# Another order of all engine queues in the expert steps of a fused attention, mixture-of-experts and FFN kernel

## The chip, the cores and the metric
The kernel runs on one core of a Trainium2 chip. The metric is the device time of one execution in microseconds. An engine takes its instructions in the order in which the program lists them: TensorE (PE, with weight loads as PEld), VectorE (DVE), ScalarE (ACT), GpSimd (POOL) and SyncE (SP), which here issues most DMA transfers. The engines meet at semaphores.

## The reference: what is computed
Three parts, all in fp32, on 4608 tokens of 512 features.

```
attn[b,h] = softmax_d(q) @ (softmax_s(k)^T @ v)            # 8 x 8 heads, 576 x 64
x = attn as 4608 x 512
e = argmax(x @ w_gate);  g = softmax(x @ w_gate)[e] * sigmoid(x @ w_output_gate)[e]
y[t] = g[t] * relu(x[t] @ w1[e[t]]) @ w2[e[t]]             # 8 experts, 512 -> 1024 -> 512
h = y @ w_in;  out = (h * cos(h)) @ w_out                  # 512 -> 2048 -> 512
```

## The kernel before, in words
Every fp32 product is made of three matmuls on a high and a low part of each operand (high x high, low x high, high x low); the low part of the hidden activations stands beside the high one. So before a weight or a token block can be used, ACT rounds it to its high part and DVE (or POOL) subtracts that to get the low one.

The kernel has three stages: attention with the router, the expert stage, and the FFN. The change is in the expert stage. After the router, the tokens are sorted by expert: DVE works out each token's position ("pos", L942 to L955), makes one-hot matrices from its low and high digits ("low", "hot", "ri": L186, L966 to L974), PE multiplies these in three groups of 12 (L978) to the list of token numbers in sorted order, and two DVE instructions ("inv", L981 and L982) make the integer list by which POOL gathers. "far" (L960 to L962) checks with one tiny matmul whether a position lies beyond a bound.

The expert stage then runs 22 steps, numbered 0 to 21, after the string "DDDHDHFDHDHDHFF". Each F is a step of 256 tokens (two blocks of 128), each D a pair of them that share one expert's weights, each H a half step of 128 tokens. That makes 17 full steps and 5 half steps: 6, 9, 13, 16 and 19 are the half ones. A step takes this way through the engines, with the lines by which the profile names it:

- weights: "ld" loads a quarter of an expert's two matrices (SP, L256), "wh" makes the high part (ACT, L264), "wl" the low one (DVE, L268; the fourth quarter for the first step, raw tile 3, on POOL);
- tokens: "gat" gathers a block of 128 (POOL, L277, two buffers), "norm" scales it (POOL, L282), "tr" transposes it (PE, L287), "xh" and "xl" make the two parts (ACT L294, DVE L299);
- first product: "mm0" and "mm1" (PE, L1141 to L1144) for each of four groups of hidden columns, "hh" the relu and high part (ACT, L1162), "hl" the low part (DVE, L1166), "hs" a sum for half steps;
- second product: "mm2" (PE, L1177 to L1179), "y" copies and stores it (ACT, L1183 and L1185).

Steps 0 and 1 gather tokens before the sort is finished, by a list known earlier; from step 2 on the gather needs "inv".

Beside this, the stage prepares the FFN's weights, which arrive as double floats and are taken apart with integer instructions: "cld" (SP load), "csq" and "clf" (ACT, L1063, L1066), "ca", "ch", "cp" (DVE, L1071 to L1079), "cm", "cs" (POOL, L1082, L1086), "cw" (DVE, L1099). From the result "wsum" (POOL, L1114) adds combinations, "whi" and "wlo" split them (ACT L1122, DVE L1126), "wst" stores them (a DMA issued by ACT, L1129).

All of this is written as a table of operations: a name, a key (a planned time in us), the function that emits the instructions, and the names of operations that have to be emitted earlier. One routine emits them: of all operations whose listed ones are out, it takes the one with the smallest key. This fixes the order of every engine's queue. Two examples of entries, "hh" and "hl" of step j and group n, and the sort's "far":

```
("far", ST["far"], s_far, "pos"),
...
op(T0 + (bt["dmm1"] * n + 0.3 if j else 0.3) if soon else t1 + bt["hh"], ("hh", j, n), ..., ("mm1", j, n), ...)
```

## Time and profile before

| | us |
|---|---|
| median of 3 runs (lowest, highest) | 1468.21 (1467.05, 1470.45) |
| the profiled execution | 1465.47 |
| its span | 1463.7 |
| attention and router, 0 to 185.06 | 185.06 |
| expert stage, 185.06 to 684.11 | 499.05 |
| FFN, 684.11 to 1463.70 | 779.59 |

The span is the time from the first to the last instruction that the profiler saw; the rest of the profiled execution's time lies around it. The expert stage is counted from the first matmul of step 0's first product to the first one of the FFN, and a step from its first such matmul to that of the next.

### The profile page before, as it was taken

Reading aid. Unit: us, or ns where it says so; the run is one execution under the profiler, and the core shown is the slowest. Engines: PE = TensorE matmul, PEld = TensorE weight load, DVE = VectorE, ACT = ScalarE, POOL = GpSimd, SP = SyncE. Lnnn points to the kernel's source line nnn. Section 1 sums busy time; section 2 is a strip of 40 time slices with the busy share of each in tenths; the row PEclk is TensorE's granted clock in tenths of the full one; section 3 lists DMA queues with packets and bytes.
Section 4 is the critical chain, followed back from the end, with each engine's and each line's share of the span. In section 5 each row is a group of like instructions: output and inputs, shape, how many; then the busy total and the mean of one; then the engine's idle time right before and its main releaser. Section 6 shows DMA issues by size and latency. Waiting matters only on the chain.

```text
span 1463.7 us, 25384 instructions
## 1 busy us (share of the span) xinstructions
PE 1396.7 (95%) x9530; PEld 1241.4 (85%) x9530; DVE 983.2 (67%) x1465; ACT 872.8 (60%) x1613; POOL 545.2 (37%) x391
## 2 busy tenths in 40 slices
PE   6898869999899999899999999999999999999998
PEld 5777759899799889799898898988889899898887
DVE  7999985777787888786655655546565554655544
ACT  3776515456464655566766666666666666666654
POOL 5555314564644463624252423406032240603000
PEclk9999889999999999999999999999999999999999
DMA  9985424767886967897667575666657566665662
GB/s 314 278 263 168 157 96 143 275 249 246 295 289 244 315 228 249 309 300 253 226 184 220 173 230 169 210 193 197 204 172 231 170 200 200 202 202 171 192 192 82
DMA packets 189731, 317.99 MB, mean 217 GB/s; under 512 B 27744, under 2 KB 60000, under 8 KB 189600
## 3 DMA queue, kind: packets, MB, share of 16 engines
q1 hardware_dynamic: 153760, 253.54, 54.9%
q10 hardware_dynamic: 29840, 42.92, 8.0%
q0 software_dynamic: 6000, 19.83, 4.2%
q8 instruction: 78, 1.28, 0.4%
q14 instruction: 53, 0.43, 0.1%
HBM read 264.17 MB, written 52.05 MB: 216 GB/s over the span
## 4 chain that ended last, share of the span: by engine, by line
PE 52%; ACT 2%; DVE 2%; issue 1%; POOL 0%; DMA 0%; ACTq 0%
PE acc L1574 8%; PE acc L1572 8%; PE acc L1573 8%; PE bank L1508 7%; PE bank L1510 7%; PE bank L1509 7%; DVE n L1542 1%; PE p L1473 1%; PE yps L1177 1%; PE yps L1178 1%; PE yps L1179 1%; DVE n L1551 1%; PE hp L1144 1%; PE hp L1141 1%; ACT n L1545 1%
## 5 line engine op out<-in xcount | busy, mean ns | idle before, releaser
L1508 PE MATMUL bank<-xo,wp 128*128 128x256 f32 x994 | 281.6, 283 | 1.5 <-ACT part L1522 0.6
L1510 PE MATMUL bank<-xo,wp 128*128 128x256 f32 x994 | 277.6, 279 | 0.0
L1509 PE MATMUL bank<-xo,wp 128*128 128x256 f32 x994 | 277.2, 279 | 0.0
L1551 DVE SCALAR_TENSOR_TENSOR n<-n,h 128x512 f32<-128x512 f32 x144 | 126.0, 875 | 171.1 <-ACT n L1548 171.1
L1572 PE MATMUL acc<-wh,ht 128*128 128x512 f32 x576 | 227.6, 395 | 0.2 <-ACT ht L1557 0.2
L1573 PE MATMUL acc<-wl,ht 128*128 128x512 f32 x576 | 227.4, 395 | 0.0
L1574 PE MATMUL acc<-wh,ht 128*128 128x512 f32 x576 | 226.8, 394 | 0.5 <-DVE ht L1561 0.5
L1508 PEld LDWEIGHTS bank<-xo,wp 128*128 128x128 f32 x994 | 186.8, 188 | 22.8 <-ACT part L1522 4.2
L1509 PEld LDWEIGHTS bank<-xo,wp 128*128 128x128 f32 x994 | 186.7, 188 | 16.2
L1141 PE MATMUL hp<-xTh,wh 128*128 128x256 f32 x704 | 187.8, 278 | 2.9 <-DVE ht L1166 2.9
L1144 PE MATMUL hp<-xTh,wl 128*128 128x256 f32 x704 | 187.4, 277 | 0.0
L1510 PEld LDWEIGHTS bank<-xo,wp 128*128 128x128 f32 x994 | 187.4, 189 | 0.0
L268 DVE TENSOR_TENSOR wl<-raw,wh 128x1024 fp32r<-128x1024 f32 x121 | 168.8, 1419 | 26.4 <-ACT wh L264 26.4
L857 POOL TENSOR_TENSOR xo<-x,xo 128x512 fp32r<-128x512 f32 x24 | 31.1, 1298 | 373.3 <-ACT xo L852 373.3
L1530 DVE TENSOR_TENSOR h<-bank,part 128x256 f32<-128x256 f32 x213 | 89.3, 421 | 111.4 <-PE bank L1510 110.4
L264 ACT CAST wh<-raw 128x1024 fp32r<-128x1024 f32 x126 | 127.5, 1053 | 42.5 <-PE yps L1179 25.8
L1537 ACT ACTIVATE n<-h 128x512 int32<-128x512 f32 x144 | 91.1, 632 | 101.4 <-DVE h L1530 97.8
L1143 PE MATMUL hp<-xTl,wh 128*128 128x256 f32 x544 | 150.8, 277 | 0.0
L1545 ACT ACTIVATE n<-n 128x512 f32<-128x512 f32 x144 | 91.2, 633 | 77.9 <-DVE n L1542 77.9
L1141 PEld LDWEIGHTS hp<-xTh,wh 128*128 128x128 f32 x704 | 132.2, 188 | 4.5 <-DVE ht L1166 3.5
L1144 PEld LDWEIGHTS hp<-xTh,wl 128*128 128x128 f32 x704 | 132.2, 188 | 0.2
L1574 PEld LDWEIGHTS acc<-wh,ht 128*128 128x128 f32 x576 | 108.3, 188 | 26.7 <-DVE ht L1561 1.4
(310 smaller groups left out, 3093.8 us busy)
## 6 DMA issues: line engine op xcount, KB each, us to landing
wp<-ws SPq DMA_DIRECT2D x504, 256.0 KB, 2.8
raw<-in_moe_w_dram SPq DMA_DIRECT2D x60, 1024.0 KB, 7.2
ws<-wst ACTq DMA_DIRECT2D x28, 512.0 KB, 6.1
...
```

The source lines that it names most:

```text
L264: sc.copy(out=wh[j, c][:, s], in_=rawt[c][:, s])
L268: eng.tensor_tensor(out=wl[j, c][:, s], in0=rawt[c][:, s], in1=wh[j, c][:, s], op=ALU.subtract)
L1141: pe.matmul(hp[:, f2, :], w_h, xTh[j][:, d, :], start=(d == 0), stop=False)
L1143: pe.matmul(hp[:, f2, :], w_h, xTl[j][:, d, :], start=False, stop=False)
L1144: pe.matmul(hp[:, f2, :], w_l, xTh[j][:, d, :], start=False, stop=(d == KD - 1))
L1508: pe.matmul(h, w[:, 0, k], x[:, i, 0, k], start=(first and k == 0), stop=False, skip_group_check=True)
L1509: pe.matmul(h, w[:, 0, k], x[:, i, 1, k], start=False, stop=False, skip_group_check=True)
L1510: pe.matmul(h, w[:, 1, k], x[:, i, 0, k], start=False, stop=(k == 1), skip_group_check=True)
L1551: ve.scalar_tensor_tensor(out=rs[j, s], in0=rs[j, s], scalar=-0.5, in1=hs[j, s], op0=ALU.add, op1=ALU.mult)
L1572: pe.matmul(acc[t, a], gh[f][:, ts], w_h, start=(c == 0), stop=False)
L1573: pe.matmul(acc[t, a], gh[f][:, ts], w_l, start=False, stop=False)
L1574: pe.matmul(acc[t, a], gl[f][:, ts], w_h, start=False, stop=(c == KF - 1))
```

## The change
A table SHIFT gives an offset to the keys, by the operation's name and its place: the kind of step (the first of a pair is "D", the second or a single one "F", a half step "H"; for token blocks and weights that of the step before; steps 0 to 2 by number) and the block, group or quarter. The offsets are added just before the operations are emitted. Since dependences that the old keys implied no longer hold by themselves, they are now listed. No instruction is added, removed or changed; the last offsets also swap the order of a few parts of the FFN's first token tile.

```
-            op(c3 + n, ("wh", 3, n), lambda n=n: whigh(0, 3, n))
+            op(c3 + n, ("wh", 3, n), lambda n=n: whigh(0, 3, n), ("wh", 3, n - 1))
...
-                   ("xl",) + (pv2 or (-1, 0)))
+                   ("xl",) + (pv2 or (-1, 0)), ("tr",) + (tiles[-2] if len(tiles) > 1 else (-1, 0)))
...
-                       ("hl", j, 2 * c + 1), ("wl", 4 * g + 2 + c, 1),
+                       ("hl", j, 2 * c), ("hl", j, 2 * c + 1), ("wl", 4 * g + 2 + c, 0), ("wl", 4 * g + 2 + c, 1),
...
-        issue(ops)
+        SHIFT = dict(
...
+            cld={('i',): -3.65, ('o',): -18.9},
...
+            hh={('0', 2): 7.8, ('1', 2): -3, ('1', 3): -36.3, ('D', 0): 0.4, ('D', 1): 4.2, ('F', 2): -72.8, ('F', 3): -45.95,
+                ('H', 3): -1.05},
...
+            norm={('1', 0): -18.3, ('1', 1): 16.25, ('D', 0): -3.75, ('F', 0): -3.2, ('H', 0): 7.1},
...
+            s={('exp',): 14.15, ('gate',): 11.85, ('hot',): 15.45, ('mm_0',): 11.05, ('more',): 13.55, ('pos',): 16.35,
+                ('px',): 2},
+            tr={('D', 0): -68.85, ('F', 0): -1.55, ('H', 0): -100.5, ('H', 1): -76.35, ('Z', 2): 0.55},
...
+        def place(n):
...
+            if t in ("gat", "norm", "tr", "xh", "xl"):
+                return ("Z" if j == NSLOT else kinds[j - 1] if j > 2 else str(j), n[2])
+            if t in ("hh", "hl", "hs", "y"):
+                return (kinds[j] if j > 1 else str(j), n[2])
+            return (j,) if t in ("oh", "ol", "xs") else ()
+
+        issue({n: (key + SHIFT.get(n[0], {}).get(place(n), 0.0), fn, deps) for n, (key, fn, deps) in ops.items()})
```

What this does to the queues is shown at three places.

First, step 0 on DVE, after the position chain: one piece of the difference. L186 are the twelve compares of "low", L960 and L961 are "far", L299 a low part of step 1's tokens, L966 to L974 the one-hots, L1166 low parts of step 0's hidden groups 2 and 3.

```order
 L186 TENSOR_SCALAR ht<-iota_b,lo_f 128x128 x12
+L960 TENSOR_SCALAR fl<-posf 128x4
+L961 TENSOR_SCALAR posN<-posf 128x4
+L299 TENSOR_TENSOR xTl<-t,xTh 128x4x128
 L966 TENSOR_TENSOR ohh<-ht,hi_b 128x36x27 x2
 L968 TENSOR_SCALAR rpi<-ohh,pcol 128x36x54
 L974 TENSOR_TENSOR rpi<-ohh,iota_b 128x36x54
-L1166 SCALAR_TENSOR_TENSOR hx<-hp,hx 128x512 x2
-L299 TENSOR_TENSOR xTl<-t,xTh 128x4x128
-L960 TENSOR_SCALAR fl<-posf 128x4
-L961 TENSOR_SCALAR posN<-posf 128x4
```

"far" now stands behind the compares and ahead of the one-hots; the low parts of groups 2 and 3 are done ahead of the position chain.

On PE in the same step, the rows around "far" (L962). Before, it stands between the first and the second of four groups of twelve second products (yps is the block's accumulator):

```order
L1178 MATMUL yps_2521<-wl_2092,hx_2413 128x512
L1179 MATMUL yps_2521<-wh_2091,hx_2413 128x512
L962 LDWEIGHTS ones_c_81
L962 MATMUL sp_2277<-fl_2538,ones_c_81 1x4
L1177 MATMUL yps_2573<-wh_2091,hx_2385 128x512
L1178 MATMUL yps_2573<-wl_2092,hx_2385 128x512
```

Now it stands behind the last of them, and the first product of step 1 follows; the sort's matmuls, which stood between the other groups, are in step 1.

```order
L1178 MATMUL yps_2499<-wl_2307,hx_2478 128x512
L1179 MATMUL yps_2499<-wh_2306,hx_2478 128x512
L962 LDWEIGHTS ones_c_81
L962 MATMUL sp_2277<-fl_2583,ones_c_81 1x4
L1141 MATMUL hp_2595<-xTh_2481,wh_1936 128x256
L1143 MATMUL hp_2595<-xTl_2482,wh_1936 128x256
```

Second, step 7 on ACT: the relus of its hidden groups 1, 2 and 3 (L1162), two high parts of the prepared FFN weights (L1122), their stores (L1129), and one conversion (L1063, L1066). Before:

```order
L1162 ACTIVATE ht_4194<-hp_4167 128x512
L1122 CAST wst_4198<-wf_3632 128x2x2x128
L1122 CAST wst_4203<-wf_3632 128x2x2x128
L1129 DMA ws_133<-wst_4198 128x2x512
L1129 DMA ws_133<-wst_4203 128x2x512
L1063 ACTIVATE sq_4239<-rw_4152 128x512
L1066 ACTIVATE rw_4152<-rw_4152 128x512
L1162 ACTIVATE ht_4270<-hp_4206 128x512
```

Now the relu of group 2 follows that of group 1 directly, and the stores come behind that of group 3:

```order
L1162 ACTIVATE ht_4215<-hp_4160 128x512
L1162 ACTIVATE ht_4244<-hp_4190 128x512
L1063 ACTIVATE sq_4247<-rw_3937 128x512
L1066 ACTIVATE rw_3937<-rw_3937 128x512
L1122 CAST wst_4258<-wf_3681 128x2x2x128
L1122 CAST wst_4263<-wf_3681 128x2x2x128
L1162 ACTIVATE ht_4266<-hp_4219 128x512
L1129 DMA ws_133<-wst_4263 128x2x512
```

Third, step 8 on POOL: a gather for the half step 9 (L277), its scaling (L282), and conversions (L1082, L1086) and a sum (L1114) of the FFN's weights. Before:

```order
L277 DMA xg_4350<-xs_64,invI_2261 128x520
L1086 TENSOR_TENSOR rw_4235<-rw_4235 128x512
L1114 TENSOR_TENSOR wsum_4378<-wf_3632 128x512
L1082 TENSOR_TENSOR rw_4321<-rw_4321,a_4384 128x512
L1086 TENSOR_TENSOR rw_4321<-rw_4321 128x512
L1114 TENSOR_TENSOR wsum_4444<-wf_3632,wsum_4318 128x512
L282 TENSOR_TENSOR xg_4350<-xg_4350 128x4x128
```

Now one conversion less and one sum less stand between gather and scaling:

```order
L277 DMA xg_4326<-xs_64,invI_2261 128x520
L1114 TENSOR_TENSOR wsum_4352<-wf_3681 128x512
L1082 TENSOR_TENSOR rw_3937<-rw_3937,a_4316 128x512
L1086 TENSOR_TENSOR rw_3937<-rw_3937 128x512
L282 TENSOR_TENSOR xg_4326<-xg_4326 128x4x128
```

The scaling moved ahead of the last conversion and of a sum, which follow behind it.

And on PE ahead of step 7: behind the last second products of the half step 6 now come the transposes of step 8's first block (L287), which stood in the middle of step 7.

```order
L1178 MATMUL yps_4073<-wl_3963,ht_4066 128x512
L1179 MATMUL yps_4073<-wh_3962,ht_4067 128x512
L287 MATMUL t_4114<-ident_68,xg_4014 128x128 x4
L1141 MATMUL hp_4124<-xTh_4056,wh_3994 128x256
L1143 MATMUL hp_4124<-xTl_4057,wh_3994 128x256
```

The same move is made for the second step of five other pairs (steps 3, 5, 12, 15 and 18), and the transposes of the step behind a half step (7, 10, 14, 17, 20) moved from its second products into the middle of its first ones.

## Rows read from the trace of the kernel before

**Rows 1.** Windows: the expert stage; columns: start:end, us, busy us (count) by engine, clock, DMA share, GB/s.
```profile
185.06:684.11 499.05, 471.47 (x3093) 421.63 (x3093) 386.48 (x510) 264.93 (x408) 231.79 (x164) 0.98 0.72 249
```

**Rows 2.** The same view by step: steps 0, 2, 7, 8, 9 and 14.
```profile
185.06:224.75 39.69, 27.25 (x192) 23.93 (x191) 31.22 (x95) 7.42 (x13) 5.90 (x4) 0.83 0.27 94
...
247.51:270.50 22.99, 22.99 (x154) 20.82 (x153) 17.64 (x24) 11.03 (x19) 13.80 (x10) 1.00 0.47 159
...
355.16:383.11 27.95, 25.03 (x154) 21.78 (x152) 26.95 (x30) 15.17 (x24) 17.77 (x10) 0.94 0.63 223
383.11:407.91 24.80, 23.04 (x150) 20.42 (x148) 17.59 (x20) 12.48 (x18) 15.49 (x12) 1.00 0.93 327
407.91:421.66 13.75, 13.75 (x98) 12.61 (x97) 10.11 (x17) 9.80 (x18) 1.94 (x2) 1.00 0.97 337
...
507.32:534.23 26.91, 23.91 (x154) 20.47 (x152) 26.02 (x29) 15.83 (x25) 18.17 (x10) 1.00 0.64 221
```

**Rows 3.** Waits of PE in the expert stage: total us, times, longest.
```profile
PE yps L1177 <- ACT ht L1162: 7.1, 3, 2.9
PE t L287 <- POOL xg L282: 3.1, 5, 0.8
```

**Rows 4.** Timeline of PE in step 0: start, us, operation, [idle before, releaser].
```profile
212.30 0.16 PE L962 MATMUL sp<-fl,ones_c 128*1 128x4 bf16 x1 [12.44 <-DVE fl L960]
...
217.32 1.34 PE L978 MATMUL sp<-rpi,ht 128*128 128x108 bf16 x24
...
221.32 0.75 PE L978 MATMUL sp<-rpi,ht 128*128 128x108 bf16 x12
```

**Rows 5.** Windows: the stretch after PE's longest idle time in step 0.
```profile
212.39:216.84 4.45, 4.45 (x12) 3.48 (x12) 3.19 (x21) 0.47 (x2) 0.00 (x0) 0.50 0.77 251
```

**Rows 6.** Timeline of DVE in step 0.
```profile
193.37 0.43 DVE L942 TENSOR_TENSOR pa<-sp,lim 128x288 f32<-128x288 f32 x1
...
197.97 2.37 DVE L953 TENSOR_SCALAR lo_i<-posI 128x12 int32<-128x12 int32 x1
...
200.37 2.28 DVE L955 CAST lo_f<-lo_i 128x12 f32<-128x12 int32 x1
...
203.34 2.02 DVE L186 TENSOR_SCALAR ht<-iota_b,lo_f 128x128 bf16<-128x128 bf16 x12
205.29 2.23 DVE L966 TENSOR_TENSOR ohh<-ht,hi_b 128x972 bf16<-128x972 bf16 x2
...
208.20 2.18 DVE L974 TENSOR_TENSOR rpi<-ohh,iota_b 128x1944 bf16<-128x1944 bf16 x1
...
212.09 0.16 DVE L960 TENSOR_SCALAR fl<-posf 128x4 bf16<-128x4 f32 x1
```

**Rows 7.** Timeline of POOL before and in step 0, and in step 1.
```profile
197.87 4.76 POOL L268 TENSOR_TENSOR wl<-raw,wh 128x1024 fp32r<-128x1024 f32 x2 [10.95 <-ACT wh L264]
...
227.22 0.98 POOL L277 DMA_INDIRECT xg<-xs,invI  x1
...
230.66 1.04 POOL L282 TENSOR_TENSOR xg<-xg 128x512 f32<-128x512 f32 x1 [1.20 <-DMA xg<-xs,invI]
```

**Rows 8.** Timelines of ACT: a relu of step 0, then step 7 (q: DMA issue).
```profile
196.25 0.60 ACT L1162 ACTIVATE hx<-hp 128x512 fp32r<-128x512 f32 x1 [2.12 <-PE hp L1144]
...
371.72 2.07 ACTq L1129 DMA_DIRECT2D ws<-wst  x2
373.83 0.68 ACT L1063 ACTIVATE sq<-rw 128x512 f32<-128x512 f32 x1 [7.93 <-DVE wst L1126]
...
374.98 0.57 ACT L1162 ACTIVATE ht<-hp 128x512 fp32r<-128x512 f32 x1
```

**Rows 9.** Timeline of DVE in step 7.
```profile
370.16 3.22 DVE L1126 TENSOR_TENSOR wst<-wf,wst 128x512 fp32r<-128x512 f32 x2
...
376.52 0.69 DVE L1126 TENSOR_TENSOR wst<-wf,wst 128x512 fp32r<-128x512 f32 x1
```

**Rows 10.** Timeline of POOL in step 8.
```profile
394.67 1.49 POOL L282 TENSOR_TENSOR xg<-xg 128x512 f32<-128x512 f32 x1
```

More of the change, by code (lines that the diff above doesn't have):

```diff
@@ L1314 @@
                      ("a", c_a, [("cm", m - 1)]), ("h", c_h, [("csq", m)]), ("p", c_p, []), ("m", c_m, [("clf", m)]),
-                     ("s", c_s, []), ("w", c_w, [("csq", m), ("wlo", f - 2, 6)]), ("hi", c_hi, [])]
+                     ("s", c_s, []), ("w", c_w, [("csq", m), *[("wlo", f - 2, i) for i in range(7)]]), ("hi", c_hi, [])]
             last = None
             for n, fn, deps in chain if kind == "o" else chain[:-1]:
-                op(t1 + CT[n], ("c" + n, m), lambda fn=fn, m=m: fn(m), *deps, *([last] if last else []))
+                op(t1 + CT[n], ("c" + n, m), lambda fn=fn, m=m: fn(m), *deps, ("c" + n, m - 1), *([last] if last else []))
                 last = ("c" + n, m)
@@ L1326 @@
                 for i, n, late in WP["part"]:
-                    op(tj[n] + WP["hi"] + late, ("whi", f, i), lambda f=f, i=i: w_high(f, i), *full,
+                    op(tj[n] + WP["hi"] + late, ("whi", f, i), lambda f=f, i=i: w_high(f, i), *full, ("wlo", f - 1, i),
                        *[("wsum", f, k) for k in range(4)][:{1: 1, 3: 2, 5: 3, 4: 4}.get(i, 0)], ("wst", f - 1, i))
@@ L1344 @@
                 if g and lead[j] == j and (slot or c < 3):
-                    free = ("wl", L - 3, 1)
+                    free = [("wl", i, n) for i in (L - 3, L - 4) for n in range(2)]
                     store = [("chi", 2 * KD * c + KD + n) for n in range(KD)] if slot is None else []
-                    op(t0 + pt[f"w{c}"] - 12.0, ("ld", L), lambda slot=slot, c=c: wload(slot, c), free, ("ld", L - 1), ("s", "eI"), *store)
+                    op(t0 + pt[f"w{c}"] - 12.0, ("ld", L), lambda slot=slot, c=c: wload(slot, c), *free, ("ld", L - 1), ("s", "eI"), *store)
                     use = ("mm1", j - 1, 2 * c + 1) if c < 2 else ("mm2", j - 1, c - 2, pa_)
                     for n in range(2):
-                        op(t0 + pt[f"w{c}"] + n * pt["dn"], ("wh", L, n), lambda j=j, c=c, n=n: whigh(j, c, n), ("ld", L), use)
+                        op(t0 + pt[f"w{c}"] + n * pt["dn"], ("wh", L, n), lambda j=j, c=c, n=n: whigh(j, c, n), ("ld", L), use,
+                           ("wh", L, n - 1))
                         op(t0 + pt[f"w{c}"] + n * pt["dn"] + pt["dl"], ("wl", L, n), lambda j=j, c=c, n=n: wlow(j, c, n, ve),
@@ L1375 @@
                 op(t1 + bt["mm1"] - (0.0 if j else 0.01), ("mm0", j, n), lambda j=j, n=n, slot=slot: mm1(j, n, slot, (0,)),
-                   ("xl", j, na - 1), ("wl", 4 * g + c, 1), ("hl",) + pm, ("mm1", j, n - 1))
+                   *[("xl", j, a) for a in range(na)], ("wl", 4 * g + c, 0), ("wl", 4 * g + c, 1), ("hl",) + pm, ("mm1", j, n - 1))
                 op(t1 + bt["mm1"] + (0.0 if j else bt["dmm1"] / 2), ("mm1", j, n),
@@ L1392 @@
             for a in range(na):
-                op(T0 + bt["y"] + bt["dmm2"] * a, ("y", j, a), lambda j=j, a=a, slot=slot: yout(j, a, slot), ("mm2", j, 1, a), ("s", "done"))
+                op(T0 + bt["y"] + bt["dmm2"] * a, ("y", j, a), lambda j=j, a=a, slot=slot: yout(j, a, slot), ("mm2", j, 1, a), ("s", "done"),
+                   ("y", j, a - 1) if a else ("y", j - 1, len(blocks(slots[j - 1])) - 1))
             T0 += LEN[kind] if j else P0["len"]
@@ L1415 @@
             op(t0 + at + 0.7, ("ol", i), lambda i=i, e2=e2: x_low(0, i, e2), ("oh", i))
-        issue(ops)
+        SHIFT = dict(
+            chi={('o',): 12.7},
+            cld={('i',): -3.65, ('o',): -18.9},
+            cm={('i',): 11.5, ('o',): 10.7},
+            cp={('o',): 3.4},
+            csq={('i',): 1.55, ('o',): 1.9},
+            cw={('i',): 3.15, ('o',): 7.6},
+            gat={('2', 1): 10.85, ('D', 0): -15.4, ('H', 1): 9.1},
+            hh={('0', 2): 7.8, ('1', 2): -3, ('1', 3): -36.3, ('D', 0): 0.4, ('D', 1): 4.2, ('F', 2): -72.8, ('F', 3): -45.95,
+                ('H', 3): -1.05},
+            hl={('1', 1): 3.05, ('1', 3): -14.1, ('D', 2): 6.4, ('F', 2): -33.3, ('F', 3): -88.65, ('H', 3): -72.1},
+            hs={('H', 0): -80.25, ('H', 1): -138.15, ('H', 2): -3.05, ('H', 3): -91.25},
+            ld={('F', 2): -13.65},
+            norm={('1', 0): -18.3, ('1', 1): 16.25, ('D', 0): -3.75, ('F', 0): -3.2, ('H', 0): 7.1},
+            oh={(3,): 3.6, (4,): 25.85, (5,): 18.6},
+            s={('exp',): 14.15, ('gate',): 11.85, ('hot',): 15.45, ('mm_0',): 11.05, ('more',): 13.55, ('pos',): 16.35,
+                ('px',): 2},
+            tr={('D', 0): -68.85, ('F', 0): -1.55, ('H', 0): -100.5, ('H', 1): -76.35, ('Z', 2): 0.55},
+            wh={('1', 0, 0): -1.8, ('1', 2, 1): 5.25, ('F', 2, 0): -20.4, ('F', 2, 1): -0.95, ('F', 3, 0): 1.1, ('F', 3, 1):
+                0.85, ('H', 0, 0): -111.6, ('H', 0, 1): -36.8, ('H', 2, 0): -0.15, ('H', 2, 1): -3.4, ('w3', 0): -45.2, ('w3',
+                1): -18.25},
+            whi={(1,): 18.9, (2,): 17.9, (5,): 17.65},
+            wl={('1', 0, 0): 4.65, ('1', 1, 0): 4.25, ('1', 2, 0): 3.35, ('F', 2, 1): 2.45, ('H', 0, 0): -164.95, ('H', 1, 0):
+                -18, ('H', 1, 1): -7.45, ('H', 2, 0): -0.25, ('H', 3, 0): -1.25, ('w3', 0): -58.35},
+            wlo={(0,): 13.55, (3,): 16.2},
+            wst={(0,): 33.95, (1,): 29.4, (2,): 22.8, (3,): 31.35, (5,): 29.6},
+            wsum={(3,): 32},
+            xh={('1', 1): 8.75, ('D', 1): 5.6, ('F', 1): 5.65, ('H', 0): -32.35},
+            xl={('2', 0): -5.75, ('F', 0): 6, ('H', 0): -44.6},
+            xs={(0,): 4.7, (3,): 3.85},
+            y={('0', 0): 7.35, ('1', 0): 10.15, ('D', 1): 12.45, ('F', 0): 1.5, ('F', 1): -47.1, ('H', 0): 11.6},
+            zero={(): 9.55},
+        )
@@ new lines, in place @@
+        def place(n):
+            t, j = n[0], n[1]
+            if t == "s":
+                return (j.rstrip("0123456789") if j.startswith("low") else j,)
+            if t in ("wh", "wl", "ld"):
+                if j == 3:
+                    return ("w3", n[2])
+                b = next(b for b in group if group[b] == j // 4)
+                return ("1" if b == 2 else kinds[b - 1], j % 4, *n[2:])
+            if t in ("cld", "csq", "clf", "ca", "ch", "cp", "cm", "cs", "cw", "chi"):
+                return (cjobs[j][1],)
+            if t in ("wsum", "whi", "wlo", "wst"):
+                return (n[2],)
+            if t in ("gat", "norm", "tr", "xh", "xl"):
[3 more added lines that the diff above has]
+            return (j,) if t in ("oh", "ol", "xs") else ()
```

8 lines of the change are left out of this document (4 added, 4 removed).

## The prediction, made before the changed kernel ran
> **What bounds the kernel now.** I read the trace by stage first. The table of windows gives each engine's busy time, the clock granted to TensorE (1.00 is 2.4 GHz, 0.50 is 1.2 GHz) and the share of the DMA engines. The FFN stage keeps its order, so I leave it out. In the expert stage PE is busy 471.47 of 499.05 us [rows 1]: 27.6 us of idle PE, and some time at the lower clock, is all that another order can win, since the number of matmuls stays.
>
> The second view is the same table cut at the first matmul of each step. Step 2 shows what a full step costs when PE never waits: 22.99 us, PE busy 22.99; a half step is 13.75, as step 9 shows [rows 2]. The stage has 17 full and 5 half steps, and the sort's 36 matmuls stand in it too (24 in 1.34 us, 12 in 0.75: 2.1 us) [rows 4]. So 17 x 22.99 + 5 x 13.75 + 2.1 = 461.7 us would be a stage with no wait, 37.4 less than it has. Where the 37.4 lie, by the step rows: step 0 has 39.69 - 22.99 - 2.1 = 14.6; step 7 has 4.96; step 14 has 3.92; step 17, which does the same work one FFN slice later, repeats step 7, so I count it as much again; all others together are 9.0, of which step 8 shows 1.8 [rows 2].
>
> The third view, PE's waits, says who is late: L1177 (second product) waits for the relu on ACT, three times, 7.1 us in all, and the transposes L287 wait for POOL's scaling, 3.1 us in five [rows 3]. The single largest wait is in step 0: L962, one tiny matmul of "far", waits 12.44 us for the DVE instruction L960 [rows 4]. PE's queue is served in order, so second products, whose inputs were ready, stand behind it. And after that idle time PE runs at clock 0.50: from 212.39 to 216.84 the next twelve matmuls take 4.45 us [rows 5]. What they cost at 1.00 follows from step 2: 96 matmuls of 256 columns, 48 of 512 and 8 short transposes in 22.99 us make about 0.115 us for the narrow and 0.23 for the wide ones, so 2.8 for twelve; 1.7 us more are lost.
>
> **Step 0, term 1.** Why is L960 late? On DVE the sort's position chain starts at 193.37 (L942) and ends after L955 at 202.65, 9.3 us; two of its instructions, L953 and L955, take 2.37 and 2.28 us where L960, on a similarly small tile, takes 0.16 [rows 6]; in just that time POOL makes the low part of the fourth weight tile, from 197.87 for 4.76 us [rows 7]. Then the twelve compares L186 (2.02 us), the sort's one-hots from L966 to L974 (205.29 to 210.38, 5.1 us), two late parts and a cast stand ahead of L960, which runs at 212.09 [rows 6].
>
> The change alters three things here. On DVE "far" goes straight behind the compares, ahead of L966. On PE L962 goes behind all four groups of second products of step 0, so that nothing of step 0 is queued behind it; the sort's matmuls go into step 1. On POOL the fourth weight's low part is split, one half ahead of the gathers for step 1, the other between them, with ACT's casts of it first in the stage; it no longer meets the end of the position chain. The cost of the new order, from rows: step 0 without the sort's matmuls lasts 22.99 us, so PE comes to L962 at 185.06 + 22.99 = 208.05. DVE starts the position chain after the fourth low part of the first product; ACT's relu for it starts at 196.25 and lasts 0.60 [rows 8]; three DVE instructions of 0.6 to 0.7 us behind it (two low parts and one low part of x) bring the start to about 198.8. The chain without the stretched pair takes 9.3 - 2.37 - 2.28 + 0.3 = 4.9 us, end 203.7; compares 2.0; L960 by about 205.9. That is 2 us ahead of PE, so the wait vanishes, and with it the slow clock: term 1 is 14.6 less what is given for reading the edges, **14.3 us**. If the chain kept its 9.3 us, L960 would come at 210.3, PE would wait about 2.3, and the term is 12. Late next: the sort's one-hots end at about 205.9 + 0.7 + 5.1 = 211.7 (0.7 for a low part of x ahead of them), the matmuls then run in step 1 at about 214, and the index list is there at some 216. The first gather by it took 3.44 us from issue (227.22) to scaling (230.66), the scaling 1.04 [rows 7]; 220.7 for the scaled block, and the transposes of step 2 come on PE at about 226. I see 0 to 1.5 us of wait for the second block.
>
> A rule bears on this. The Trainium skill, "GPSIMD Engine Reference", section "1. Specifications", says that POOL shares its SBUF interfaces with VectorE and contends with DVE instructions that have two SBUF inputs or run in a two-port mode. This trace agrees in L953 and L955 above. By it the two-input compares of the expert list, now beside the moved half tile, would stretch by as much as the 2.4 us that half of 4.76 lasts, the position chain would start 1 to 2.4 later and term 1 would be some 13.5 rather than 14.3.
>
> **Steps 7, 14, 17, term 2.** Here ACT's queue is the cause. In step 7 two DMA issues of the rearranged FFN weights (L1129) end at 373.8; the next ACT instruction had idled 7.93 us for DVE's L1126; the relu of the third hidden part stands behind these and runs only at 374.98 [rows 8]. That pair of L1126 took 3.22 us beside POOL's work, 1.6 each, where one alone takes 0.69 [rows 9]. In the new order the third relu follows the second directly, ahead of L1122 and L1129, so it needs only the first product, done some 8 us earlier. The DMA issues go into the next steps, into an ACT that is busy 12.48 of step 8's 24.80 us [rows 2]. What remains is DVE: it is busy 26.95 of 27.95 us in step 7 [rows 2], and the third low part needs a turn there before PE reaches the last two groups. The pieces that the shifts push out of this step (two to three L1126 and one L1099 or so) are worth 2 to 4 us of DVE, so a clean step of 22.99 would still ask for about 23 to 25 us of it unless what stretches it goes too. I take a residue of 1 us in each of steps 7 and 17: 9.9 - 2 = **8**. Bounds: 9.9 if DVE's stretch goes with POOL's overlap, 3 if PE's wait of 2.9 only turns into one for DVE, with the slow clock still there. Step 14 has the same form with a smaller wait: 3.9 less 1.4, **2.5** (0 to 3.9).
>
> **The rest, term 3.** In steps like 8 the transposes wait for POOL's scaling [rows 3]: at 394.67 it runs after a conversion (L1082, L1086) and a sum (L1114) [rows 10]. The new order puts it ahead of the second conversion and sum, whose own reader is DVE a step later; 1.3 + 1.0 + 1.3 us earlier is enough for single waits of at most 0.8. Of 9.0 us I take **4**: steps 8, 12 and 18 nearly whole, nothing of the parts that are slower matmuls or the FFN's first transposes in step 21. Bounds 0 and 9.
>
> **New waits, term 4.** In six pairs the first transposes of the second step now stand ahead of the first step's matmuls, and behind a half step both transposes stand within its first products. Behind a transpose the whole of PE waits. Time from the transposes that free the buffer to those that need it: behind a half step 32 matmuls of the first and 24 of the second product, about 32 x 0.115 + 24 x 0.23 = 9.2 us; in a pair 24 to 48 second products, 5.6 to 11. The gather and its scaling need 3.44 + 1.04 = 4.5 [rows 7], or 4.9 with the 1.49 of step 8 [rows 10]. That fits, by 0.7 us in the tightest. I subtract **2.5** for the tight one, the second block of step 2 and SP's changed load order; bounds 0 and 8.
>
> The sum: 14.3 + 8 + 2.5 + 4 - 2.5 = 26.3 us. The profiled execution took 1465.47 (its span is 1463.7); 1439.2 in its terms. The median of the runs shown is 2.7 higher, so the forecast is **1442**. If all 37.4 went it would be 1431.
>
> **Rivals.**
> A, *DVE takes the stall over*. Step 0 is cured, but in steps 7, 14 and 17 PE waits for DVE's low part instead of ACT's relu, with the slow clock again, and the new waits eat term 3. Saves 12 to 14 less 1 or so, near 12: 1456. For it: DVE's 26.95 of 27.95. Against: the last wait named in step 7 is ACT's, and DVE work moves out of the step too.
> B, *no gain*. The index list is the true end of step 0's chain: if the one-hots and the matmuls behind "far" come 8 us later than I have it, the gathers of step 2 are late, and PE idles in step 2 what it saved in step 0. 1468. Against: some 5 us of slack by the numbers above, and only what exceeds it counts.
> C, *slower: transposes that meet late gathers*. Six pairs and five half steps have a transpose pulled ahead. DMA engines are busy 0.93 and 0.97 in steps 8 and 9 [rows 2]; a gather that lands late stops PE, and the clock falls as in step 0, 1.7 us each. It decides from a gather and scaling of some 10 us on: at the three pairs with 9.2 us to spend that costs 0.8 us and the clock, at the tight one 4.4. Six pairs that each lose 3.7 us and 1.7 for the clock lose 32, more than the 26 won: 1442 + 32 = 1474. Against: the landing seen, in the same stage.
>
> **How the numbers follow.** Main case 0.65, its own range 1434 to 1450 (the sum with step 0 at 12 and term 2 at 3 to 10). A 0.20, B 0.06, C 0.09. The range 1431 to 1461 holds the main case and A and leaves out B and C, 0.15. A change of 0.2% (2.9 us) is about what a measurement of this kernel can tell from none; so faster is 0.65 + 0.20 = 0.85, same 0.06, slower 0.09.
>
> **What would show it.** Step 0 should last about 23 us, with L962 without a wait and at a clock of 1.00; step 1 about 25, as it takes the sort's matmuls. In steps 7 and 17 the wait of L1177 for ACT should be gone, the step 23 to 25 us, and the clock 1.00. Scaling in step 8 should no longer end a wait of L287. The expert stage should be some 473 us. I am wrong if L962 still waits over 3 us, if step 2 grows by more than 3, if L1166 takes L1162's place as the one that PE waits for in steps 7, 14 and 17, or if L287 waits over 2 us in steps 3 to 18.

## The result and the profile after

The changed kernel takes 1453.15 us (median of 4 runs, 1451.31 to 1454.04) against 1467.68 for the kernel before in the same runs: a ratio of 0.9896, 95% interval 0.9879 to 0.9913, some 14 to 15 us faster. The forecast was 1442 with a range of 1431 to 1461: the direction and the range hold, the size does not; a good 26 us were forecast, and the main case's own range, 1434 to 1450, is missed. The profiled execution has a span of 1450.7 us, 13.0 less than before.

The windows of the changed kernel, by the first matmul of each step, answer to [rows 1] and [rows 2]: the whole expert stage, then steps 0, 1, 2, 6, 7, 8, 9, 14, 17 and 21, then the FFN.

```profile
183.00:668.79 485.79, 473.62 (x3103) 427.15 (x3104) 373.58 (x511) 261.44 (x402) 231.22 (x165) 0.99 0.73 257
183.00:209.18 26.18, 25.84 (x168) 22.54 (x168) 21.63 (x70) 5.21 (x8) 9.06 (x6) 1.00 0.30 101
209.18:237.66 28.48, 25.54 (x194) 22.78 (x193) 22.71 (x45) 14.05 (x21) 11.77 (x10) 1.00 0.57 205
237.66:261.89 24.23, 24.23 (x152) 22.01 (x150) 13.78 (x21) 11.03 (x19) 14.16 (x12) 0.93 0.43 129
330.78:349.05 18.27, 16.02 (x101) 14.58 (x100) 12.45 (x17) 11.68 (x20) 6.42 (x6) 0.91 0.92 337
349.05:372.08 23.03, 23.03 (x152) 20.87 (x150) 20.91 (x25) 12.45 (x21) 14.95 (x11) 1.00 0.38 131
372.08:394.62 22.54, 22.54 (x150) 20.32 (x148) 18.81 (x23) 11.70 (x17) 12.38 (x9) 1.00 0.93 321
394.62:413.27 18.65, 15.64 (x98) 14.21 (x97) 12.54 (x18) 11.35 (x20) 5.80 (x5) 0.91 1.03 384
497.39:520.01 22.62, 22.62 (x151) 20.47 (x150) 21.21 (x26) 11.38 (x19) 13.90 (x10) 1.00 0.62 206
557.39:580.42 23.03, 23.03 (x152) 20.82 (x150) 21.33 (x23) 15.75 (x25) 13.63 (x10) 1.00 0.41 144
641.89:668.79 26.90, 24.77 (x161) 21.93 (x160) 15.81 (x16) 13.90 (x19) 10.71 (x8) 1.00 0.66 238
668.79:1450.69 781.90, 771.79 (x4881) 689.47 (x4879) 435.41 (x675) 495.60 (x981) 218.72 (x154) 1.00 0.64 192
```

Steps 7, 14 and 17 are what was forecast or better. Step 0, forecast at 23 us, is 26.2 from its first matmul, because some of the router's matmuls now stand between the first and the second part of its first product (the second part starts at 186.95); from there it takes 22.2, with PE never idle. New are the half steps 6 and 9: 18.27 and 18.65 us, where step 9 took 13.75 before [rows 2] and step 6 as much, with PE idle 2.3 and 3.0 us in them and a clock of 0.91. Step 1 and step 2 are longer, so is step 21, and the FFN has 2.2 us more than its 779.7 (counted here from its first matmul, at 683.95 before; the 684.11 of [rows 1] lies 0.16 us behind it).

PE's waits in the stage, the answer to [rows 3] (total, times, longest):

```profile
PE hp L1141 <- DVE ht L1166: 5.3, 2, 3.0
PE t L287 <- POOL xg L282: 3.5, 3, 2.3
PE t L1210 <- POOL yg L1205: 1.5, 1, 1.5
```

L1177's wait for ACT and L962's for DVE are gone. In their place PE waits in the *first* product of the half steps, twice, for a low part on DVE.

Where the time went, as the difference of two profiled executions:

| | before | after | difference |
|---|---|---|---|
| attention, to the second part of step 0's first product | 186.5 | 187.0 | +0.4 |
| from there to step 1 (the sort's 36 matmuls, 2.1 us by [rows 4], move out) | 38.2 | 22.2 | -16.0 |
| steps 1 and 2 (those 2.1 us move in) | 45.8 | 52.7 | +7.0 |
| steps 7, 14 and 17 | 82.8 | 68.7 | -14.1 |
| half steps 6, 9, 13, 16, 19 | 68.8 | 80.1 | +11.3 |
| step 21 | 23.9 | 26.9 | +3.0 |
| the other steps | 238.0 | 231.2 | -6.7 |
| FFN | 779.7 | 781.9 | +2.2 |

### The profile page after: what moved, and what is told of

Same layout as the page of the kernel before. It is cut to its first block, busy times and chain, and to the rows that moved or that the text cites. A ratio compares the mean times of both kernels' runs of the same rounds, so it can differ in the third digit from the quotient of the medians.

```text
span 1450.7 us, 25366 instructions
## 1 busy us (share of the span) xinstructions
PE 1399.1 (96%) x9530; PEld 1247.3 (86%) x9530; DVE 970.9 (67%) x1465; ACT 871.9 (60%) x1613; POOL 545.9 (38%) x391
## 4 chain that ended last, share of the span: by engine, by line
PE 78%; DVE 11%; DMA 4%; ACT 4%; issue 2%; POOL 0%; ACTq 0%; SPq 0%; DVEq 0%; POOLq 0%
PE acc L1629 8%; PE acc L1628 8%; PE acc L1627 8%; PE bank L1563 7%; PE bank L1565 7%; PE bank L1564 7%; PE hp L1141 5%; PE hp L1144 5%; PE hp L1143 4%; PE yps L1177 4%; PE yps L1178 4%; PE yps L1179 4%; DVE m L384 2%; DMA raw<-in_moe_w_dram 1%; PE xp L527 1%
## 5 line engine op out<-in xcount | busy, mean ns | idle before, releaser
L1141 PE MATMUL hp<-xTh,wh 128*128 128x256 f32 x704 | 193.7, 285 | 5.8 <-DVE ht L1166 5.3
L1144 PE MATMUL hp<-xTh,wl 128*128 128x256 f32 x704 | 192.1, 282 | 0.0
L268 DVE TENSOR_TENSOR wl<-raw,wh 128x1024 fp32r<-128x1024 f32 x121 | 164.6, 1379 | 11.2 <-ACT wh L264 10.6
L1629 PEld LDWEIGHTS acc<-wh,ht 128*128 128x128 f32 x576 | 108.3, 188 | 26.8 <-DVE ht L1616 1.7
```

Source lines behind the costliest of these rows:

```text
L268: eng.tensor_tensor(out=wl[j, c][:, s], in0=rawt[c][:, s], in1=wh[j, c][:, s], op=ALU.subtract)
L1141: pe.matmul(hp[:, f2, :], w_h, xTh[j][:, d, :], start=(d == 0), stop=False)
L1144: pe.matmul(hp[:, f2, :], w_l, xTh[j][:, d, :], start=False, stop=(d == KD - 1))
L1629: pe.matmul(acc[t, a], gl[f][:, ts], w_h, start=False, stop=(c == KF - 1))
```

## The half steps: what ACT waited for

On ACT ahead of step 6 (a q behind the name is a DMA issue), and the load on SP that the last row's releaser names:

```profile
330.98 0.59 ACT L1183 COPY yt<-yps 128x512 f32<-128x512 f32 x1 [1.27 <-PE yps L1179]
336.25 0.34 ACTq L1185 DMA_DIRECT2D ys<-yt  x1
336.63 0.37 ACT L1152 COPY ht<-hp 128x256 f32<-128x256 f32 x1 [5.07 <-DMA raw<-in_moe_w_dram]
```

```profile
326.23 0.37 SPq L256 DMA_DIRECT2D raw<-in_moe_w_dram  x1
```

```profile
raw<-in_moe_w_dram SPq DMA_DIRECT2D x1, 1024.0 KB, 9.9
```

The last row is the DMA view of that one load: 9.9 us to landing, so it lands at about 336.2. The copy of step 5's result ends at 331.57, but its store is issued only at 336.25, and all of step 6 on ACT (L1152, L1162, the casts) stands behind it. The store does not read what the load brings. The trace shows the tie: the operands of each issue name the semaphore that tells of its landing. All 827 transfers that SP and ACT issue share eight semaphores, given out in turn in the program's order, and not one is issued before the last user of its semaphore has landed; an issue whose semaphore is still taken waits. These are the eight "slots" of the expectations below. The stretch in the program's order, with the time of issue, the semaphore and the landing:

```
326.23 SP  L256  raw <- w1    semaphore 107   336.17
325.44 ACT L1129 ws <- wst    semaphore 109   332.84
326.70 SP  L1058 rw <- w_in   semaphore 100   337.92
327.64 SP  L1058 rw <- w_out  semaphore 101   339.22
328.65 ACT L1129 ws <- wst    semaphore 102   336.71
328.92 SP  L1058 rw <- w_out  semaphore 103   340.78
329.74 ACT L1185 ys <- yt     semaphore 104   338.47
332.47 SP  L256  raw <- w1    semaphore 105   345.08
336.25 ACT L1185 ys <- yt     semaphore 107   waits for the first row
```

So at most eight such transfers are on their way in this trace, and a store on ACT can hang on a load of SP. The change's SP order puts three FFN weight loads (semaphores 100, 101, 103) and two weight stores (109, 102) into this stretch. Step 9 has the same form: a weight store of ACT is issued at 396.71 when a load issued at 387.85 lands (8.8 us, semaphore 109), and a result store at 400.80 when one from 392.07 does (8.7, semaphore 101). Ahead of the half step 16 a result store waits 2.4 us behind its copy, again for a load.

## The experiments

All times stand beside runs of the kernel before on the same chip. "Stage" is the time from the second part of step 0's first product to the FFN's first product: 497.4 us before, 481.8 with the change. It is read from one profiled execution of each kernel. The attention ahead of it, which the experiments alter only at its very end, took 186 to 197 us in the profiled executions, so steps and stages are compared, and totals by their intervals.

**e1: one transfer more.** The direct test of the tie: the queues stay, only the pairing shifts by one.

```
+        def spacer():
+            t = LB["ca"].tile([1, 8], F32, tag="sp8", name="sp8")
+            sy.dma_start(out=t, in_=w_gate[0:1, 0:8])
+        op(123.06, ("spacer", 0), spacer, ("ld", 16))
```

> The changed kernel with one 32-byte load more in SP's queue, ahead of the three FFN weight loads that stand before the store of step 5's second block; no other queue changes. Theory 'slots': each SP or ACT transfer carries one of eight completion semaphores in turn, and its issue waits until the transfer eight places earlier has landed; the store of step 5 then stood behind a weight load that lands at 336.17, and one transfer more in between pairs it with a store that lands at 332.84. ACT's idle time there falls from 4.7 us to 1.0 to 1.5, the half step 6 from 18.3 us to 14 to 15, PE's wait of 2.25 us for DVE in it is gone; step 9 keeps its 18.7. In all 3 to 4 us faster than the changed kernel, about 1449. Rival 'queue order': step 6 is long because the low parts stand behind weight work on DVE and ACT; then nothing changes, 1453, step 6 stays at 18.

Measured: 1452.82 us, ratio 0.9901 (0.987 to 0.9933), span 1447.9, stage 478.8. ACT ahead of step 6, and the windows of steps 6 and 9:

```profile
331.79 0.59 ACT L1183 COPY yt<-yps 128x512 f32<-128x512 f32 x1 [0.71 <-PE yps L1179]
333.64 0.34 ACTq L1185 DMA_DIRECT2D ys<-yt  x1
```

```profile
331.59:345.83 14.24, 14.24 (x101) 13.09 (x100) 10.34 (x15) 7.75 (x15) 7.06 (x6) 1.00 1.04 404
393.70:409.30 15.60, 14.03 (x98) 12.76 (x96) 9.87 (x16) 11.41 (x20) 6.11 (x5) 1.00 1.04 378
```

The store waits 1.3 us instead of 4.7, as worked out: its semaphore is now 109, which a weight store of ACT frees at 333.56. Step 6 takes 14.24 us with PE never idle: a load of 32 bytes wins 4 us there. That settles the tie and refutes the rival for step 6. Step 9 changed too, which was not expected: a wait of 2.7 us for a slot is left to read there, and for the other the landing is not recorded. Elsewhere some microseconds were lost again (the wait at step 3's transposes grew to 3.4, step 16 to 15.7), so the total, forecast at 1449, is not clearly better than the changed kernel's.

**e4: the result stores on SP.** `sc.dma_start` of L1185 becomes `sy.dma_start`.

> The changed kernel with the stores of the expert steps' results issued by SP instead of ACT. Theory 'slots': an issue that has to wait for a slot then holds up SP, whose loads are early, and not ACT, whose casts PE needs within the step: the half steps 6 and 9 fall from 18.3 and 18.7 us to about 14 to 15.5 (a weight store of ACT still waits some 5 us ahead of step 9), 5 to 8 us faster than the changed kernel, 1445 to 1448. Rival: SP now waits for ACT's copies, the next weights come late, and steps 7 to 21 grow: 1453 or more.

Measured: 1456.74 us, ratio 0.9928 (0.9903 to 0.9953), stage 482.0. Steps 6, 9, 10 and 21:

```profile
329.72:343.83 14.11, 14.11 (x101) 12.97 (x100) 9.49 (x15) 7.98 (x16) 4.45 (x4) 1.00 1.04 402
391.12:405.00 13.88, 13.88 (x97) 12.80 (x96) 9.81 (x15) 7.85 (x15) 3.45 (x3) 1.00 1.04 387
405.00:431.24 26.24, 23.61 (x157) 21.20 (x156) 20.00 (x22) 16.96 (x22) 10.24 (x8) 1.00 0.96 335
637.99:668.20 30.21, 24.24 (x161) 21.44 (x160) 19.45 (x20) 17.50 (x26) 14.50 (x11) 0.98 0.54 180
```

Both half steps are clean, as the theory says. The total is not better: step 10 and step 21 lose 2.9 and 3.3 us against the changed kernel, and the FFN 3.5. So the theory holds for the place, the rival for the sum.

**e2 and e3: the opening alone, and all but the opening.** A filter in front of the offsets:

```
+        FIRST = {"s": None, "wh": "w3", "wl": "w3", "hh": "0", "y": "0", "norm": "1", "xh": "1"}
+        def opening(n):
+            return n[0] in FIRST and (FIRST[n[0]] is None or place(n)[0] == FIRST[n[0]])
...
+        issue({n: (key + (SHIFT.get(n[0], {}).get(place(n), 0.0) if opening(n) else 0.0), fn, deps)
```

> The offsets of the sort, of the fourth weight tile and of step 0's relus and stores and step 1's scaling and casts alone; all other offsets 0. If the step 0 part is worth what the trace of the changed kernel shows (its end comes 15.6 us earlier, of which 2.1 are the sort's matmuls, now in step 1), about 13 us are won less 0 to 4 of new waits in steps 1 and 2: 1455 to 1459, with steps 7, 14 and 17 still near 28, 27 and 28 us and steps 6 and 9 at 13.8. Rival: the index list comes too late without the other offsets, step 2's gather stalls, and less than 6 us are won.

> The complement: step 0 as before, all other offsets as in the change. By the step rows of the changed kernel steps 3 to 5, 7, 8, 10 to 12, 14 and 17 win about 20 us and steps 6, 9, 13, 18 and 21 lose about 14, and the FFN 2: 4 to 6 us won, about 1463. If the losses in the half steps hang on how transfers are paired in the eight slots, they may be elsewhere or gone, since fewer microseconds precede them but the order of transfers is the same: then 1455 to 1460. Rival: without the early start the rest gives nothing, 1467.

Measured, e2: 1459.87 us, just above its 1455 to 1459, ratio 0.994 (0.9917 to 0.9963), stage 487.3, with steps 7, 14 and 17 at 27.6, 28.1 and 28.0 us and steps 6 and 9 at 14.0 and 13.8. Step 1 meets a wait of 1.3 us at the transposes of step 2's second block, step 2 is clean. e3: 1468.47, ratio 0.9991 (0.9969 to 1.0014), not told from before and near the 1467 of its rival; its stage is 493.3, 4.2 less, but the half steps 6, 9 and 16 take 18.4, 19.0 and 16.2. The opening gives 10.1 of the 15.6 us that the change takes off the stage; what the rest wins in steps 7, 14 and 17 it loses in the half steps. So the half steps' losses do not come from the early start.

**e5, e10 and e6: the FFN weights' split alone, all but it, and it with the opening.** The filters name the operations:

```
+        ... if n[0] in ("wsum", "whi", "wlo", "wst") else 0.0        # e5
+        ... 0.0 if n[0] in ("wsum", "whi", "wlo", "wst") else ...    # e10
```

> Of all offsets only those of the FFN weights' sums, splits and stores (wsum, whi, wlo, wst); everything else in the old order. Theory: the 28, 27 and 28 us of steps 7, 14 and 17 come from these operations' place on ACT and DVE alone, so the three fall to 23 to 24 each, 12 to 13 us won less what the moved work costs elsewhere, 1456 to 1460, and the half steps 6 and 9 stay at 13.8, since few transfers crowd ahead of their stores. Rival: the relus and low parts need their own offsets too (or the moved work only stalls the next steps as it did these); then less than 5 us, over 1464.

> The change without the offsets of wsum, whi, wlo and wst. If these four alone relieve steps 7, 14 and 17, the three go back to some 27 to 28 us, 12 us in all, and the kernel to 1462 to 1466, though the half steps 6 and 9 may change, since other transfers then stand ahead of their stores. Rival: the early relus, low parts and weight parts of the other offsets do it; then the three stay under 25 us.

> The offsets of the opening (as in e2) and of wsum, whi, wlo, wst together, and none of the rest: no transposes, token scalings, weight parts or loads pulled. If the two are independent their stage gains add: 10 for the opening, 12 for the split, so some 22 us off the expert stage against 15.6 for the whole change, and the FFN keeps its 779.7 us: 1446, 6 to 7 faster than the changed kernel. This is the version that should beat both. Rival: the gains of the steps overlap, as the moved work lands in steps that the opening has made tight; then no better than the changed kernel, 1452 to 1455.

Measured: e5 1466.95 (ratio 0.9994, 0.9978 to 1.0009), stage 497.6; e10 1471.16 (1.0015, 1.0 to 1.003), stage 497.8; e6 1454.03 (0.9896, 0.9881 to 0.991), stage 485.1. In e5 steps 7, 14 and 17 take 24.6, 24.8 and 26.8 us, and step 10 takes the work: 

```profile
417.25:445.39 28.14, 23.83 (x153) 21.08 (x152) 20.24 (x22) 16.09 (x21) 9.91 (x7) 1.00 0.77 276
```

PE's waits for the low parts in e5:

```profile
PE hp L1141 <- DVE ht L1166: 6.9, 5, 2.3
PE yps L1179 <- DVE ht L1166: 5.7, 6, 1.6
```

In e10 steps 7, 14 and 17 take 27.0, 25.8 and 27.0, and two of the steps behind them are worse, step 8 with 32.1 and step 18 with 29.3. Steps 7 and 8 of e10, and PE's waits in its stage:

```profile
354.05:381.09 27.04, 24.33 (x152) 21.45 (x150) 24.30 (x28) 14.00 (x24) 18.41 (x13) 0.94 0.52 175
381.09:413.21 32.12, 25.54 (x149) 23.11 (x148) 19.36 (x22) 11.25 (x17) 12.27 (x9) 0.89 0.79 277
```

```profile
PE hp L1141 <- DVE ht L1166: 10.2, 2, 6.6
PE yps L1179 <- DVE ht L1166: 6.9, 4, 2.7
```

So both totals miss, and in e5 the rival holds. The split offsets are needed (e10), but alone they only carry much of the stall some steps on (e5). In both, the wait for ACT is nearly gone (1.1 us left in e10, none in e5) and PE waits for DVE's low parts instead: in e10 2.7 and 2.6 us in steps 7 and 17 themselves. In the changed kernel steps 7, 8, 10, 11 and 12 are clean together; which of the other offsets that needs was not tried. e6 was to beat both kernels and equals the changed one, as its rival said: the split, worth nothing alone (stage 497.6), takes 2.2 us off e2's stage, and by the two ratios some 6 us off its total.

The two groups also say where other losses belong. e10's half steps take 72.7 us in all, e5's 71.7, against 80.1 with the change: their loss needs the split's stores and the other offsets together. Step 21 takes 23.9 us in e2 and in e10, without the split's offsets, and 25.5 and 26.0 in e5 and e6, which have them and leave the end of the stage as it was. The FFN takes 779.3 to 780.3 in e2, e5 and e6, and 781.5 to 781.6 in e1, e3, e8 and e10, which have the remaining offsets too.

**e7: the scalings as well.** e6 with `or (n[0] == "norm" and n[1] > 2)` in the filter.

> As e6, with the offsets of the token blocks' scaling on POOL (norm, steps 2 to 21) too. If the waits of L287 for POOL's scaling in steps 3, 8, 12 and 18 (0.5 to 0.9 us each) are due to its place behind conversions and sums, they go and 1 to 3 us more are won than in e6, mostly in steps 8, 12 and 18; rival: the gather lands late anyway and nothing changes.

Measured: 1462.45, ratio 0.9954 (0.9937 to 0.9971), stage 492.4. The transposes' waits in steps 3, 8, 12 and 18 are gone, but in e6 only step 12's (0.95 us) was left of them, so the scalings can claim no more than that. Steps 11 and 12 take 23.0 and 22.5 us, but step 10 takes 31.5 and step 14 28.6 (25.9 and 25.4 in e6), with PE waiting there for DVE's weight and low parts. Added to e6, this one group of offsets costs more than it wins.

**e8: one offset back.** The transposes of step 3's first block at their old key.

```
+ (0.0 if n == ("tr", 3, 0) else SHIFT.get(n[0], {}).get(place(n), 0.0))
```

> The changed kernel with one offset taken back: the transposes of step 3's first block stand again within step 2, not ahead of its matmuls. Theory: they stop all of PE for 2.3 us at the start of step 2, and the slow clock behind that costs 1.2 more; steps 1 and 2 together fall from 52.7 to about 49.5, and the kernel by about 3 us, 1450. Rival: the wait only moves to the second block of step 2 or later, steps 1 and 2 stay over 51.5.

Measured: 1446.13, ratio 0.9842 (0.9823 to 0.9861), clearly under the changed kernel's 0.9896. Steps 1 and 2 of e8:

```profile
213.60:238.83 25.23, 25.17 (x189) 22.73 (x189) 20.02 (x42) 12.06 (x19) 9.18 (x8) 1.00 0.60 210
238.83:261.81 22.98, 22.98 (x153) 20.81 (x152) 17.90 (x23) 13.03 (x21) 18.24 (x13) 1.00 0.52 182
```

48.2 us against 52.7: transposes moved too early cost 4.5. The whole stage of e8 is 479.5, only 2.3 less than with the change, since step 0 from its second part and step 8 take 1.5 us more each; the profiled execution is the slowest of its five, and the rest of the gain in the total is not placed. The same place in the changed kernel, POOL's gather and scaling and PE's transposes:

```profile
228.88 0.95 POOL L277 DMA_INDIRECT xg<-xs,invI  x1 [1.55 <-PE t L287]
...
236.09 1.10 POOL L282 TENSOR_TENSOR xg<-xg 128x512 f32<-128x512 f32 x1 [2.07 <-DMA xg<-xs,invI]
```

```profile
237.24 0.68 PE L287 MATMUL t<-ident,xg 128*128 128x128 f32 x4 [2.27 <-POOL xg L282]
```

The gather takes 7.2 us from issue to scaling here, where the forecast took 3.44 [rows 7]. Three loads of SP are issued within 1.2 us ahead of it, from 227.74 to 228.77.

**e9, e11, e12: what was lost, taken back.** Keys set one by one; e9 has e1's load too.

```
+        OWN = {("tr", 3, 0): 0.0, ("y", 19, 0): 0.0, ("wst", 1, 0): 38.0, ("wst", 1, 1): 33.0, ("zero", 4): 12.5}
+        def shift(n):
+            if n in OWN:
+                return OWN[n]
+            return 0.0 if n[0] in ("oh", "xs") or place(n) == ("Z", 2) else SHIFT.get(n[0], {}).get(place(n), 0.0)
```

e11 has of OWN only ("y", 19, 0) and no extra load; e12 is e9 with ("y", 20, a) and ("y", 21, a) at 0.0 too.

> The change with what the runs so far lay its losses to taken back: the transposes of step 3's first block stand in step 2 again, one small load more in SP's queue ahead of step 6 (as in e1), two stores and a clearing store of ACT (wst 1 0, wst 1 1, zero 4) stand behind the result stores of step 8, so that these are paired with earlier transfers, step 19's result store and the order of the FFN's first token tile (oh, xs, the third transposes) are as before the change. If the losses are separate: steps 1 and 2 win 4, step 6 wins 4, step 9 wins 4, step 21 2 to 3, the FFN 2 against the changed kernel, 16 in all, 1437 to 1440. Rival: what one place gives goes into the next (as in e1, where steps 8, 10, 13 and 16 grew), and 1446 to 1450 is reached, no better than e8.

> The change with only the end of the stage as before: the offsets of oh, xs and the third transposes of the FFN's first tile, and of step 19's result store, taken back. If the FFN's 781.9 us (779.7 before) and step 21's 26.9 (23.9) come from these, they fall to about 779.7 and 24 to 25, 4 to 5 us faster than the changed kernel, 1448 to 1449. Rival: step 21 waits for the gathers because the stage as a whole is tighter; then it stays over 26, and only the FFN's 2 us come back.

> e9 with the result stores of steps 20 and 21 at their old keys too, so that the end of the stage is as before the change altogether. In e9 the FFN's first product waited 2.1 us for ACT's copy of step 21's result, which had come behind the casts of the FFN's first token tile, and the FFN took 784.6 us instead of the 779.7 of before. If that is the whole of it, the FFN returns to 779.5 to 780.5 and the kernel gains 4 to 5 us on e9, 1438 to 1440; rival: the FFN's extra time comes from its loads or from the tile's late sums, then it stays over 783 and the kernel at 1443.

Measured: e9 1443.05, ratio 0.9835 (0.9813 to 0.9858), stage 468.4, 13.5 less than with the change. Its steps 1, 6, 9 and 21, and its FFN:

```profile
209.91:235.55 25.64, 24.97 (x189) 22.54 (x189) 20.33 (x43) 11.94 (x19) 9.48 (x8) 1.00 0.58 204
327.81:341.93 14.12, 14.12 (x102) 12.98 (x100) 9.48 (x15) 7.75 (x15) 4.73 (x4) 1.00 1.04 404
389.76:403.65 13.89, 13.89 (x97) 12.81 (x96) 10.42 (x17) 10.76 (x19) 4.29 (x3) 1.00 1.04 390
632.04:656.57 24.53, 24.09 (x162) 21.51 (x160) 15.75 (x18) 15.38 (x22) 9.38 (x6) 1.00 0.71 256
```

```profile
656.57:1441.20 784.63, 773.20 (x4881) 690.97 (x4879) 435.79 (x674) 494.31 (x978) 218.83 (x154) 1.00 0.63 192
```

Every place wins what was laid to it (steps 1 and 2 take 48.6), but the FFN loses 2.7 us more: that part of the expectation is wrong, and so the total, forecast at 1437 to 1440. e11 (1457.1, ratio 0.991, 0.9881 to 0.994) shows it too, with an FFN of 784.6 us and a step 21 of 25.6, and misses its 1448 to 1449. In both, the FFN's first product waits 2.1 us for ACT's copy of step 21's result. e12 shows that these copies are the cause: with those of steps 20 and 21 at their old keys the FFN takes 780.4, as expected. Of the 4.2 us this wins, the wait itself, still 1.1, is only 1.0. Its total, 1445.68 (0.9841, 0.9815 to 0.9867), shows no gain on e9, where 1438 to 1440 was expected; in its profiled execution the attention took 10 us more than in that of the kernel before, and step 16 again waited for a slot (16.2 us). e8, e9 and e12 beat both kernels, and can't be told from each other by their totals.

## Why the prediction was right, and where it was wrong

**Term 1, step 0: right.** Forecast 14.3; measured 16.0 less 2.1 for the moved matmuls, 13.9, and 14.0 in e2. PE and DVE in step 0 of the changed kernel:

```profile
209.08 0.17 PE L962 MATMUL sp<-fl,ones_c 128*1 128x4 bf16 x1
```

```profile
192.80 1.77 DVE L994 TENSOR_TENSOR be<-bs,fh 1x24 f32<-1x24 f32 x1
...
200.48 0.45 DVE L942 TENSOR_TENSOR pa<-sp,lim 128x288 f32<-128x288 f32 x1
...
205.31 0.17 DVE L955 CAST lo_f<-lo_i 128x12 f32<-128x12 int32 x1
...
207.47 0.17 DVE L960 TENSOR_SCALAR fl<-posf 128x4 bf16<-128x4 f32 x1
```

L955 takes 0.17 us instead of the 2.28 of [rows 6], the chain 5.0 instead of 9.3. L960 came at 207.5 instead of the 205.9 worked out, still 1.6 us ahead of PE. The 1.7 us between L942 and the 198.8 forecast have a row: L994 takes 1.77 us for 24 elements, where it took 0.17 before (at 189.51), and the whole list of experts (L994 to L1001) 5.2 us instead of 2.7; POOL's half weight tile runs beside it from 192.11 to 194.52, and a scaling from 194.67. That is the stretch which the Trainium skill's "GPSIMD Engine Reference", section "1. Specifications", lets one expect of a shared interface; the trace agrees, and 13.5, the estimate by it, was as near as mine. The index list was done at 217.2, against some 216 worked out.

That the stretch comes from POOL, and not from the DVE instructions that showed it in [rows 6], can be read in e5, which has the old order of step 0. There POOL's pair starts 0.9 us later, L953 and L955 take 0.17 us each, and the next ones on DVE are long instead, L1006 1.85 for 0.17 and the compares L186 4.17 for 2.02:

```profile
198.76 4.69 POOL L268 TENSOR_TENSOR wl<-raw,wh 128x1024 fp32r<-128x1024 f32 x2 [11.44 <-ACT wh L264]
```

```profile
198.37 0.17 DVE L953 TENSOR_SCALAR lo_i<-posI 128x12 int32<-128x12 int32 x1
...
199.34 1.85 DVE L1006 CAST eI<-ef 1x31 int32<-1x31 f32 x1
201.11 4.17 DVE L186 TENSOR_SCALAR ht<-iota_b,lo_f 128x128 bf16<-128x128 bf16 x12
```

So the chain alone was 4.3 us shorter, but the stretch, 3.8 us of it, still stood ahead of L960, and L962 waited 11.5 us. One reading of the rows was wrong without touching the sum: behind the one-hots three low parts stand ahead of L960, not two and a cast.

**Term 2, steps 7, 14 and 17: right in size, half right in cause.** Forecast 10.5; measured 14.1, of which about 1 is the next steps' transposes, moved ahead. The residue that I left for DVE did not show: ACT's relu of group 2 runs directly behind its matmuls, and the low part was in time.

```profile
357.81 0.60 ACT L1162 ACTIVATE ht<-hp 128x512 fp32r<-128x512 f32 x1 [1.48 <-PE hp L1144]
```

DVE's busy time in step 7 fell from 26.95 us to 20.91, more than the 2 to 4 that were counted. But the forecast took the relu's place on ACT for the cause. e5 and e10 show that this is not enough: DVE is nearly as full, and with only the split or only the rest moved rival A happens, in e10 in steps 7 and 17 themselves and in the step behind, in e5 in part there and in part three steps on.

**Term 3, the rest: within its bounds, the cause only in part.** 4 forecast, 6.7 measured. Steps 8, 12 and 18 win 2.3, 2.4 and 0.6 us. Of the scaling's waits there, those of steps 8 and 18 are gone in e6 too, whose scalings keep their old keys; and before the change PE waited in the same three steps 1.2, 1.2 and 0.6 us for DVE's low part L1166, a wait that the forecast did not name and that is gone as well (total, times, longest, of before):

```profile
PE hp L1141 <- DVE ht L1166: 2.9, 3, 1.2
```

**Term 4, new waits: wrong.** The step that failed is "I subtract **2.5**", with bounds of 0 and 8. Measured: 4.9 in steps 1 and 2 (7.0 less the 2.1 moved in), 11.3 in the half steps (of which some 1 are transposes moved in), 3.0 in step 21, 2.2 in the FFN, 21.4 in all. Three things were missed. The tightest pair was given 0.7 us to spare, but the gather was priced by one row, 3.44 us, and took 7.2: the mechanism of rival C, at one place of its eleven. PE's 2.27 us there also meet one of the signs of being wrong, over 2 us for L287 in steps 3 to 18. The largest loss has a mechanism that no part of the forecast had: an ACT store that waits for a semaphore slot held by a late weight load (e1, e4). I had counted SP's changed load order into a lump sum instead of following who else shares its completion semaphores; the rows of before could have shown that ACT issues wait for such landings. In step 8 a weight store, its cast done at 382.65, is issued at 385.70, 0.08 us after its semaphore is freed, and the next ACT instruction names the load:

```profile
385.70 0.37 ACTq L1129 DMA_DIRECT2D ws<-wst  x1
386.11 0.68 ACT L1063 ACTIVATE sq<-rw 128x512 f32<-128x512 f32 x1 [3.46 <-DMA raw<-in_moe_w_dram]
```

And the end of the stage was taken as unmoved. Of step 21's loss 1.5 to 2.1 us go with the split's offsets (e5 and e6 against e2 and e10); how is not shown. The FFN's goes with the offsets that are neither the opening's nor the split's. That late result copies can cost it is shown for e9 (e12); in the changed kernel its first products wait 0.9 us for ACT's partial sums and 0.9 for DVE's low part of the first tile, which no run took back alone.

**The range.** 1453 lies in 1431 to 1461, but above the main case's 1450. Term 4 cost 19 us more than forecast, terms 2 and 3 gave 6 more, and the range reaches past 1450 only to take in rival A, whose mechanism did not decide. That the number still lies inside is in part luck.

**The rivals.** A's time, 1456, is nearest to the measured 1453, but not by its mechanism: the wait for L1166 that took the place of the old ones stands in the half steps and comes from ACT. B did not happen. C happened once.
